# Windowed attention and routed experts on one core: ninth-block loads moved up, one transpose moved, weight splits deferred while routing

## The chip, the core and the metric

The kernel runs on one core of a Trainium2 chip. PE is the matrix engine, DVE the vector engine, ACT the scalar engine, POOL the GpSimd engine, SP the engine that issues most loads and stores. The metric is device time in microseconds of one execution; the time before is the median of three.

## The reference

Attention first: 8 batches, 8 heads, 576 positions, head size 64; a position sees itself and the 63 before it. Its output, as 4608 rows of 512, goes through a skipping mixture of 8 experts. In short:

```
scores = q @ k.T / 8, masked to 0 <= row - column < 64; attn = softmax(scores); x = attn @ v
compute = x @ w_skip > 0; rows without it are passed through
expert  = argmax(x @ w_gate); gate = softmax value of that expert
out     = x + gate * (relu(x @ w1[expert]) @ w2[expert])
```

## The kernel before, in words

**Attention.** The 576 positions of a batch are nine blocks of 64. A tile is two blocks, 128 rows; a pair of batches makes nine tiles, and the ninth of them (tiles 8, 17, 26, 35) holds the two ninth blocks. k, q and v come in groups of four blocks, half a group per load (`load_k`, `load_q`, `load_vm`); the ninth blocks of a pair come in loads of their own: two of k (`load_k_tail`, tile `kt`), one of q (`load_q_tail`, tile `qt`, L211) and one of v (`load_v_tail`, tile `vt`). Per tile PE does the scores (`score`, L244), the transposes of the softmax (`transpose_p`, L279), the product with v (`tile_out`, av, L368), the transposes of the result x (`transpose_x`, px, L323, copied to xt by ACT at L325) and the gate's logits (`logits`, L335, written over px and copied by ACT to lg, L342). DVE masks and reduces the scores and normalises x (L379 to L382), ACT makes the exponentials, POOL masks ptm. The loop over t issues score(t+1), the transposes of x of an earlier tile, and tile_out(t-1).

**Loads.** `when_at` gives each load a tile number and one of four slots in it; `feed` puts the loads of a slot in a queue, pending, when the program comes to it. `tick` counts PE's instructions; every 256 of them (BLOCK) it issues the stores of finished tiles and then up to four loads (LOADS) from pending on SP, all made to wait for that PE instruction. These are the batches spoken of below. `after_load` bounds the transfers in flight to six.

**Routing.** When the logits of a group of tiles are done (the last group is tiles 30 to 35), `route` works on it in steps that `routes` takes from the list `late`: DVE steps (gmx, gd, gfi, gfm, goh, gohb), a count by PE into a tile pr, more DVE steps, and then one scatter of list entries per tile on POOL (L553), issued by `pace`. The lists of the third item and those after it are read when all scatters have landed (`load_list`), and their rows gathered (`gather_x`, L579).

**Experts.** Rows are worked in items, each in four steps of an up product in two halves (`up`, tile p1, L797 to L799) and, two steps later, a down product (`down`). A half's result goes through ACT (hh, L843) and DVE (hl, L846). p1, px, pt and pr share one PSUM tag with two banks, taken in turn. Rows of an item are transposed in `split_x` (px2, L786; xh by ACT, xl by DVE, L790). Weights come as pieces of 128 x 1024: a raw load (L730) into one of six buffers, then a split into whi (ACT, L749) and wlo (DVE, L750); a load reuses its buffer after the wlo six pieces before. `weights_to(n)` splits up to piece n and issues the raw loads that this frees. `expert_chunk` is one call of the expert work: it first splits some weights and then takes the next chunk (a half of an up, a half of a down, or an empty one at the end of a step). Its `need` is the last piece that the next step wants. The calls are numbered here from the first one after tile_out(34). In the seam (L1068 to L1094) they alternate by hand with the last tiles of attention, and from L1258 on with the last routing steps:

```
need = max(when[part(min(k + 1, last), 0)], when[part(min(k - 1, last), 1)] if k else 0) + 1
turns[0] += 1
more = turns[0] % 2 if late else RATE
weights_to(max(need, min(ptr["split"] + more, ptr["free"] + min(RING, len(ring)) - 1)))
```

Of the kernel before, what the change touches and what calls it, by code (L numbers as in the profile page):

```python
# [24 lines left out]
NT = N // P  # L25
# [35 lines left out]
RATE = 1  # L61
# [78 lines left out]
def window_attention_moe(ctx: ExitStack, tc, a, out):  # L140
# [171 lines left out]
    def block_v(b, i):  # L312
        if i == 8:
            return vms["t", b // 2][:, b % 2]
        return vms[2 * b + i // 4][:, i % 4]
# [3 lines left out]
    def transpose_x(t):  # L319
        x = xns.pop(t)  # L320
        px = psum.tile([P, NDC, P], F32, name="px", tag="t", bufs=2)
        for c in range(NDC):
            tick(2, nc.tensor.transpose(px[:, c], x[:, c * P : (c + 1) * P], ident))  # L323
        xt = xs.tile([P, NDC, P], F32, name="xt", bufs=NXT)
        nc.scalar.copy(xt, px)  # L325
        xts[t] = px, xt

    def logits(t):

        px, xt = xts.pop(t)  # L330
        o = px[:, 0, 0:9]
        for c in range(NDC):
            for hf in range(2):
                r = slice(64 * hf, 64 * hf + 64)
                tick(4, nc.tensor.matmul(  # L335
                    o[r], xt[:, c, r], wg[:, c], start=c == 0, stop=c == NDC - 1, skip_group_check=True
                ))
        if t in heads:
            n = GRP[heads.index(t)]
            grp[:] = [t, n, sm.tile([P, n, 9], F32, name="lg")]  # L340
        t0, n, lg = grp
        nc.scalar.copy(lg[:, t - t0], o)  # L342
        if t + 1 == t0 + n:
            late.append(route(t0, n, lg))

    def tile_out(t):
        blks = tiles[t]
        ptm = pts.pop(t)
        have = {}
        for b, i in blks:  # L350
            for w in range(2):
                if i >= w and (b, i - w) not in have:
                    have[b, i - w] = block_v(b, i - w)
        win = [[have.get((b, i - w)) for w in range(2)] for b, i in blks]
        x = xs.tile([P, D], F32, name="x")
        av = pav.tile([P, 2, 512], F32, name="av")
        summing = held[0] == "sums" and (t < 26 or held[1] >= 2)
        if summing:
            held[2] = av[:, 0, 4 * VW :]
            step()  # L360
        for q in range(4):
            for w in range(2):
                for hf in range(2):
                    if win[hf][w] is None:
                        continue
                    for z in range(2):
                        h = slice(64 * z, 64 * z + 64)
                        ins = tick(4, nc.tensor.matmul(  # L368
                            av[64 * hf : 64 * hf + 64, z, q * VW : (q + 1) * VW],
                            ptm[h, q, 2 * hf + 1 - w],  # L370
                            win[hf][w][h, q],
                            start=w == 0,
                            stop=w == 1 or win[hf][1] is None,
                            skip_group_check=True,
                        ))
        feed(t + 1, 2)
        r = sm.tile([P, 2, 4], F32, name="r")
        src = av[:, :, : 4 * VW].rearrange("p z (h c) -> p z h c", c=VW)
        nc.vector.tensor_scalar(r, src[..., 64], 1e-9, None, op0=ALU.add)  # L379
        nc.vector.reciprocal(r, r)  # L380
        stores.append((x, blks))
        beat(nc.vector.tensor_tensor(  # L382
            x.rearrange("p (q z c) -> p z q c", z=2, c=64),
            src[..., 0:64],
            r.unsqueeze(3).to_broadcast([P, 2, 4, 64]),
            op=ALU.mult,
        ))
        feed(t + 1, 3)
        xns[t] = x
        progress[0] = t + 1  # L390
        while t >= NT - 2 and stores:
            store()
        return step if summing else lambda: None
# [3 lines left out]
    def store(ins=None):  # L397
        x, ((b0, i0), (b1, i1)) = stores.pop(0)
        r0 = b0 * S + i0 * 64
        r1 = b1 * S + i1 * 64  # L400
        if r1 == r0 + 64:
            done = [nc.sync.dma_start(out[r0 : r0 + P], x)]
        else:
            done = [nc.sync.dma_start(out[r0 : r0 + 64], x[:64]), nc.sync.dma_start(out[r1 : r1 + 64], x[64:])]
        if ins is not None:
            behind(done[0], ins)
            flying.append((done[0].ins, 1))
# [86 lines left out]
    def tick(n, ins):  # L494
        pe[0] += n
        if pe[0] >= pe[1]:
            pe[1] += BLOCK
            while len(stores) > SDELAY:
                store(ins)
            transfers(ins)  # L500
        return ins
# [15 lines left out]
    def beat(ins):  # L517
        beats[0] = ins.ins
# [16 lines left out]
    def feed(t, slot):  # L535
        pending.extend(at.get((t, slot), ()))
        if pe[0] < BLOCK:
            transfers()
# [133 lines left out]
    late = []  # L672
# [3 lines left out]
    def step():  # L676
        held[:2] = next(late[0], late), 0
        if held[0] is late:
            late.pop(0)
# [18 lines left out]
    part = lambda k, w: (ITEMS[steps[k][0]][2], steps[k][1], w)  # L698
# [7 lines left out]
    when = {pc: n for n, pc in enumerate(pieces)}  # L706
    ring, used = [], {}
# [12 lines left out]
    RING = 10  # L720
    ptr = {"dma": 0, "split": 0, "free": 0, "use": 0}
    wrow = {}

    def weight_dma(n):
        e, qi, w = pieces[n]
        if e not in wrow:
            r = e % E
            ix = perm[0:1, r, 2:3] if r < 2 else tables["order"][0:1, r, 1:2]
            wrow[e] = nc.values_load(ix, engines=[SP], min_val=0, max_val=(E - 1) * NQ * P)
        return nc.sync.dma_start(  # L730
            raws[n % NRAW], a["wq"][bass.ds(wrow[e] + qi * P, P), w * 1024 : w * 1024 + 1024]
        )
# [13 lines left out]
    def weight_split(n):  # L746
        hi, lo = ring[n % RING]
        raw = raws[n % NRAW]
        nc.scalar.copy(hi, raw)  # L749
        nc.vector.tensor_tensor(lo, raw, hi.bitcast(F32), op=ALU.subtract)  # L750

    def weights_to(n):
        n = min(n, len(pieces), ptr["free"] + len(ring))
        while ptr["split"] < n:
            while ptr["dma"] < min(len(pieces), ptr["split"] + NRAW):
                if not can_load(ptr["dma"]):
                    break
                weight_dma(ptr["dma"])
                ptr["dma"] += 1
            if ptr["dma"] == ptr["split"]:  # L760
                break
            weight_split(ptr["split"])
            ptr["split"] += 1
        while ptr["dma"] < min(len(pieces), ptr["split"] + NRAW) and can_load(ptr["dma"]):
            weight_dma(ptr["dma"])
            ptr["dma"] += 1
# [3 lines left out]
    def can_load(n):  # L770
        return pieces[n][0] % E < 2 or "order" in tables
# [207 lines left out]
    with tc.manual_schedule():  # L979
# [16 lines left out]
        def when_at(t, slot, f, *args):  # L996
            at.setdefault((max(t, 0), slot), []).append(functools.partial(f, *args))
# [3 lines left out]
                part2 = i // 2 % 2 if i < 4 else i - 4  # L1001
                when_at(max(first_of[n] - AHEAD, 0) + i // 3, (0, 1, 3)[i % 3], f, n, 2 * part2, 2 * part2 + 2)
        for m in range(B // 2):
            t = 9 * m + (0 if m else 2)
            when_at(t, 3, load_k_tail, m, 0)
            when_at(t + 1, 3, load_k_tail, m, 1)
            when_at(t + 2, 3, load_q_tail, m)
            when_at(t + 3, 3, load_v_tail, m)
        for t in U0:
            when_at(t, 1, weight_dma_first)  # L1010
        score(0)
# [42 lines left out]
        hpool["h"] = ml  # L1054
        chunks = expert_chunks()
        place = [0]
        turns = [0]

        def expert_chunk():
            k = place[0]  # L1060
            last = len(steps) - 1
            need = max(when[part(min(k + 1, last), 0)], when[part(min(k - 1, last), 1)] if k else 0) + 1
            turns[0] += 1
            more = turns[0] % 2 if late else RATE
            weights_to(max(need, min(ptr["split"] + more, ptr["free"] + min(RING, len(ring)) - 1)))
            place[0], c = next(chunks)

        for j, tag in enumerate("gu"):  # L1068
            its[0].split(*xhl[0], j, tag)()
        summed = tile_out(NT - 2)  # L1070
        transpose_x(NT - 3)
        logits(NT - 3)
        summed()
        pace(1)
        expert_chunk()
        masks = transpose_p(NT - 1)
        transpose_x(NT - 2)
# [7 lines left out]
        routes(1)  # L1085
        pace(1)
        expert_chunk()
        transpose_x(NT - 1)
        routes(1)
        expert_chunk()  # L1090
        logits(NT - 1)
        routes(1)
        pace(1)
        expert_chunk()  # L1094
        attn.close()
        pattn.close()
        banks["v"] = ctx.enter_context(tc.tile_pool(name="plv", bufs=1, space=PSUM, side="right", reuse_waits="tile"))
# [169 lines left out]
        while True:  # L1267
            k = place[0]
            i, qi = steps[min(k, len(steps) - 1)]
# [17 lines left out]
    more = nc.values_load(tables["left"][0:1, 0:1], min_val=0, max_val=NSLOT)  # L1287
# [71 lines left out]
```

## Time and profile before

| | us |
|---|---|
| median of three runs | 435.95 |
| the three runs | 432.66, 435.95, 436.6 |
| the profiled execution, its own device time | 433.25 |
| its span, first to last instruction | 431.6 |

The profile has one page (busy times, the span in slices, the chain that ended last, groups of instructions) and views of the trace: timelines of an engine with the idle time ahead of an instruction and what ended it in brackets, waits in total, and windows with busy times and the clock that PE was granted (1.00 is 2.4 GHz, 0.50 is 1.2 GHz). Times count from the span's start.

### The profile page before, as it was taken

To read this page: it belongs to the slowest core of one execution; us is meant where nothing else is said; L and a number is where in the kernel's file an instruction comes from. 1 tells how busy PE (TensorE), PEld (TensorE's weight loads), DVE (VectorE), ACT (ScalarE), POOL (GpSimd) and SP (SyncE) were. 2 spreads that over 40 slices of the span, in tenths; PEclk is the share of its full clock that TensorE was granted. 3 is DMA by queue.
4 is the path that set the end of the run, shared out by engine and by line. 5 is a ranking of instruction groups with operands and counts; after the bars stand their busy time and mean duration, and the time that the engine had idled before them with its cause. 6 is when DMAs were issued, how large, how long until landed. Compare 5 with 4: busy or idle time off the path is not lost.

```text
span 431.6 us, 14543 instructions
## 1 busy us (share of the span) xinstructions
PE 393.1 (91%) x5865; PEld 341.4 (79%) x5865; DVE 271.9 (63%) x558; ACT 223.0 (52%) x658; POOL 181.7 (42%) x223
## 2 busy tenths in 40 slices
PE   5887999998989888889999899999999999999980
PEld 3775888887878777877887798898898888888860
DVE  2664678878899567679216679665455466756520
ACT  3774787676758566655124536234244444444510
POOL 4552554566765584645264717025025332101010
PEclk9997999999989899999999999999999999999995
DMA  8967879879687697748557837555758776686300
GB/s 257 315 211 238 278 241 334 261 246 320 202 269 231 190 350 252 244 151 272 207 171 234 277 116 259 166 177 183 246 191 246 240 229 200 224 269 226 93 31 18
DMA packets 40757, 95.66 MB, mean 222 GB/s; under 512 B 7401, under 2 KB 9063, under 8 KB 40680
## 3 DMA queue, kind: packets, MB, share of 16 engines
q1 hardware_dynamic: 33040, 78.17, 55.6%
q0 software_dynamic: 5056, 10.02, 7.0%
q10 hardware_dynamic: 2592, 6.52, 4.5%
q8 instruction: 47, 0.77, 0.8%
q14 instruction: 22, 0.18, 0.1%
HBM read 80.55 MB, written 14.97 MB: 221 GB/s over the span
## 4 chain that ended last, share of the span: by engine, by line
PE 77%; DVE 7%; DMA 6%; issue 4%; ACT 2%; POOLq 0%; SPq 0%; ACTq 0%; DVEq 0%
PE p L797 9%; PE p L798 8%; PE p L799 8%; PE av L368 7%; PE ps L244 7%; PE px L323 4%; PE yv L797 4%; PE yv L799 4%; PE yv L798 4%; PE pt L279 4%; PE px L335 3%; PE yw L797 3%; PE yw L798 3%; PE yw L799 3%; DVE wlo L750 2%
## 5 line engine op out<-in xcount | busy, mean ns | idle before, releaser
L750 DVE TENSOR_TENSOR wlo<-raw,whi 128x1024 fp32r<-128x1024 f32 x72 | 87.8, 1225 | 23.8 <-ACT whi L749 23.5
L843 ACT ACTIVATE hh<-p 128x256 fp32r<-128x256 f32 (+4 forms) x64 | 25.0, 390 | 111.1 <-PE p L799 106.5
L797 PE MATMUL p<-xh,whi 128*128 128x256 f32 (+5 forms) x256 | 77.0, 301 | 2.7 <-DVE hl L846 2.4
L798 PE MATMUL p<-xl,whi 128*128 128x256 f32 (+5 forms) x256 | 75.3, 294 | 0.1
L799 PE MATMUL p<-xh,wlo 128*128 128x256 f32 (+5 forms) x256 | 75.1, 293 | 0.0
L749 ACT CAST whi<-raw 128x1024 fp32r<-128x1024 f32 x72 | 74.5, 1047 | 0.0
L286 POOL TENSOR_TENSOR ptm<-pm,mask 128x512 f32<-128x512 f32 x36 | 45.8, 1272 | 56.7 <-ACT pm L285 54.3
L269 ACT ACTIVATE s<-ps,nmx 128x64 f32<-128x64 f32 x288 | 66.4, 324 | 1.2
L846 DVE SCALAR_TENSOR_TENSOR hl<-p,hh 128x256 fp32r<-128x256 f32 (+4 forms) x64 | 27.3, 427 | 59.4 <-ACT hh L843 31.9
L872 POOL DMA_INDIRECT out<-yo,les x15 | 15.2, 1014 | 103.1 <-DVE yo L871 93.2
L797 PEld LDWEIGHTS p<-xh,whi 128*128 128x128 f32 x256 | 48.3, 189 | 6.1 <-DVE hl L846 3.0
L368 PE MATMUL av<-vm,ptm 64*64 64x65 f32 x2048 | 46.1, 228 | 7.4 <-issue 7.2
L553 POOL DMA_INDIRECT lists<-ent,gdi x36 | 40.6, 1129 | 24.8 <-issue 12.8
L368 PEld LDWEIGHTS av<-vm,ptm 64*64 64x64 f32 x2048 | 39.7, 139 | 13.8 <-issue 13.1
L798 PEld LDWEIGHTS p<-xl,whi 128*128 128x128 f32 x256 | 48.4, 189 | 1.4 <-DVE xl L790 0.5
L799 PEld LDWEIGHTS p<-xh,wlo 128*128 128x128 f32 x256 | 48.4, 189 | 0.0
L244 PE MATMUL ps<-k,q 64*64 64x128 f32 (+1 forms) x1024 | 40.3, 286 | 1.8 <-issue 1.7
L260 DVE COPY_PREDICATED ps<-sel,ps 128x512 f32<-128x512 int32 x36 | 25.0, 694 | 23.3 <-PE ps L244 23.1
L325 ACT COPY xt<-px 128x512 f32<-128x512 f32 x36 | 21.2, 588 | 28.5 <-PE px L323 28.4
L244 PEld LDWEIGHTS ps<-k,q 64*64 64x64 f32 x1024 | 31.3, 143 | 3.8 <-issue 3.4
L797 PE MATMUL yv<-whi,hh 128*128 128x512 f32 (+1 forms) x72 | 28.9, 402 | 0.0
L799 PE MATMUL yv<-whi,hl 128*128 128x512 f32 (+1 forms) x72 | 28.4, 394 | 0.0
(179 smaller groups left out, 735.1 us busy)
## 6 DMA issues: line engine op xcount, KB each, us to landing
raw<-wq SPq DMA_DIRECT2D x72, 512.0 KB, 5.1
vm<-vp SPq DMA_DIRECT2D x32, 260.0 KB, 5.4
q<-qT SPq DMA_DIRECT2D x32, 256.0 KB, 4.5
out<-x SPq DMA_DIRECT2D x32, 256.0 KB, 4.4
k<-kT SPq DMA_DIRECT2D x24, 256.0 KB, 4.5
w<-wq ACTq DMA_DIRECT2D x12, 512.0 KB
k<-kT SPq DMA_DIRECT2D x8, 384.0 KB, 4.5
kt<-kT SPq DMA_DIRECT2D x8, 256.0 KB, 3.3
```

Source lines behind the costliest of these rows:

```text
L244: tick(4, nc.tensor.matmul(ps[64 * hf : 64 * hf + 64, z, p, 64 * w.start :], q[h, p], k[h, w, p], start=True, stop=True, skip_group_check= ...
L260: nc.vector.copy_predicated(cur, sel.unsqueeze(1).unsqueeze(1).to_broadcast([P, 2, 4, 64]), ps[..., :64])
L269: nc.scalar.activation(s[:, q, z], cur[:, z, q], AF.Exp, bias=nmx[:, z, q : q + 1], scale=0.125)
L286: nc.gpsimd.tensor_tensor(part(0, 2), split(pm[:, 0:2], 2), kept(2), op=ALU.mult)
L368: ins = tick(4, nc.tensor.matmul(av[64 * hf : 64 * hf + 64, z, q * VW : (q + 1) * VW], ptm[h, q, 2 * hf + 1 - w], win[hf][w][h, q], start= ...
L553: ins = nc.gpsimd.indirect_dma_start(out=lists, out_offset=bass.IndirectOffsetOnAxis(ap=di, axis=0), in_=ent.bitcast(I32), in_offset=None, ...
L749: nc.scalar.copy(hi, raw)
L750: nc.vector.tensor_tensor(lo, raw, hi.bitcast(F32), op=ALU.subtract)
L797: nc.tensor.matmul(o, lh, rh, start=first, stop=False)
L798: nc.tensor.matmul(o, lh, rl, start=False, stop=False)
L799: nc.tensor.matmul(o, ll, rh, start=False, stop=last)
L846: beat(nc.vector.scalar_tensor_tensor(hl[:, f, :m], p1[:, :m], 0.0, hh[:, f, :m].bitcast(F32), op0=ALU.max, op1=ALU.subtract))
```

## The change

Three edits. The loads of the first pair's ninth blocks get due times 1, 2, 2, 3 in place of 2, 3, 4, 5. In the seam the transposes of x of tile 33 are issued ahead of tile_out(34), and an expert call that stood behind the logits of tile 35 is issued two places earlier, so that the calls from the third on stand: third, fourth, transposes of x of tile 35, fifth, logits of tile 35. And while routing is unfinished, a call splits the pieces that its own chunk needs, or one more than are split as long as that is no more than `need`.

```diff
         for m in range(B // 2):
-            t = 9 * m + (0 if m else 2)
-            when_at(t, 3, load_k_tail, m, 0)
-            when_at(t + 1, 3, load_k_tail, m, 1)
-            when_at(t + 2, 3, load_q_tail, m)
-            when_at(t + 3, 3, load_v_tail, m)
+            ts = [9 * m + i for i in range(4)] if m else [1, 2, 2, 3]
+            when_at(ts[0], 3, load_k_tail, m, 0)
+            when_at(ts[1], 3, load_k_tail, m, 1)
+            when_at(ts[2], 3, load_q_tail, m)
+            when_at(ts[3], 3, load_v_tail, m)
...
-            turns[0] += 1
-            more = turns[0] % 2 if late else RATE
-            weights_to(max(need, min(ptr["split"] + more, ptr["free"] + min(RING, len(ring)) - 1)))
+            if late:
+                now = max(when[part(min(k, last), 0)], when[part(k - 2, 1)] if k >= 2 else 0) + 1
+                weights_to(max(now, min(need, ptr["split"] + 1)))
+            else:
+                weights_to(max(need, min(ptr["split"] + RATE, ptr["free"] + min(RING, len(ring)) - 1)))
             place[0], c = next(chunks)
 
         for j, tag in enumerate("gu"):
             its[0].split(*xhl[0], j, tag)()
+        transpose_x(NT - 3)
         summed = tile_out(NT - 2)
-        transpose_x(NT - 3)
         logits(NT - 3)
...
         expert_chunk()
+        expert_chunk()
         transpose_x(NT - 1)
         routes(1)
         expert_chunk()
         logits(NT - 1)
         routes(1)
         pace(1)
-        expert_chunk()
         attn.close()
```

## Rows read from the trace of the kernel before

**Rows 1.** The page, part 1: engine, busy us, share of the span, instructions.

```profile
PE 393.1 (91%) x5865; PEld 341.4 (79%) x5865; DVE 271.9 (63%) x558; ACT 223.0 (52%) x658; POOL 181.7 (42%) x223
```

**Rows 2.** Timeline of PE, 35 to 49 us: start, duration, engine, line, instruction.

```profile
35.15 0.64 PE L335 MATMUL px<-wg,xt 128*64 128x9 f32 x16
38.95 1.99 PE L244 MATMUL ps<-kt,qt 64*64 64x128 f32 x32 [3.16 <-DMA qt<-qT]
...
45.03 1.09 PE L244 MATMUL ps<-k,q 64*64 64x128 f32 x32
...
48.74 1.10 PE L244 MATMUL ps<-k,q 64*64 64x128 f32 x32
```

**Rows 3.** Windows: length, busy us by engine, granted clock, DMA share, GB/s.

```profile
38.00:40.00 2.00, 1.05 (x20) 1.05 (x24) 0.00 (x0) 0.00 (x0) 0.00 (x0) 0.50 0.64 214
...
44.00:46.00 2.00, 2.00 (x81) 1.79 (x74) 1.06 (x3) 1.41 (x8) 1.33 (x2) 0.98 0.89 339
```

**Rows 4.** Timeline of SP's queue, 23 to 36 us.

```profile
23.17 0.35 SPq L402 DMA_DIRECT2D out<-x  x1
...
33.90 2.00 SPq L211 DMA_DIRECT2D qt<-qT  x1
```

**Rows 5.** Waits of the whole span: us in total, times, longest.

```profile
PE av L368 <- issue: 7.2, 10, 1.4
```

**Rows 6.** Timeline of PE, 141 to 149 us.

```profile
141.91 0.58 PE L368 MATMUL av<-vm,ptm 64*64 64x65 f32 x23 [1.33 <-issue]
...
142.98 1.95 PE L244 MATMUL ps<-k,q 64*64 64x128 f32 x32
...
148.32 1.10 PE L244 MATMUL ps<-k,q 64*64 64x128 f32 x32
```

**Rows 7.** Timeline of PE, 168 to 218 us.

```profile
168.41 0.64 PE L335 MATMUL px<-wg,xt 128*64 128x9 f32 x16 [0.68 <-ACT xt L325]
...
176.97 0.66 PE L323 MATMUL px<-ident,x 128*128 128x128 f32 x4 [1.01 <-DVE x L382]
...
179.88 0.39 PE L797 MATMUL p<-xh,whi 128*128 128x256 f32 x1 [0.27 <-ACT lg L342]
...
181.42 0.60 PE L786 MATMUL px<-ident,xg 128*128 128x128 f32 x4
...
185.42 0.39 PE L797 MATMUL p<-xh,whi 128*128 128x256 f32 x1 [1.75 <-DVE hl L846]
...
203.37 0.40 PE L797 MATMUL p<-xh,whi 128*128 128x288 f32 x1 [0.67 <-DVE hl L846]
...
217.75 0.60 PE L786 MATMUL px<-ident,xg 128*128 128x128 f32 x4
```

**Rows 8.** Timeline of ACT, 167 to 177 us.

```profile
167.77 0.59 ACT L325 COPY xt<-px 128x512 f32<-128x512 f32 x1
...
176.01 0.17 ACT L342 COPY lg<-px 128x9 f32<-128x9 f32 x1 [1.29 <-PE px L335]
```

**Rows 9.** Timeline of DVE, 182 to 203 us.

```profile
182.04 0.42 DVE L846 SCALAR_TENSOR_TENSOR hl<-p,hh 128x256 fp32r<-128x256 f32 x1
182.38 0.20 DVE L424 SCALAR_TENSOR_TENSOR gfi<-gd,cf 128x48 f32<-128x48 f32 x1
...
183.22 0.68 DVE L790 TENSOR_TENSOR xl<-px,xh 128x512 fp32r<-128x512 f32 x1
183.82 1.22 DVE L750 TENSOR_TENSOR wlo<-raw,whi 128x1024 fp32r<-128x1024 f32 x1
...
199.50 3.49 DVE L750 TENSOR_TENSOR wlo<-raw,whi 128x1024 fp32r<-128x1024 f32 x3
```

**Rows 10.** Timeline of POOL, 182 to 215 us: scatters to the lists, a gather of rows.

```profile
182.74 0.97 POOL L553 DMA_INDIRECT lists<-ent,gdi  x1 [1.55 <-DVE gfi L424]
184.01 1.86 POOL L553 DMA_INDIRECT lists<-ent,gdi  x1 [0.30 <-DVE xl L790]
...
214.09 1.09 POOL L579 DMA_INDIRECT xg<-out,les  x1 [0.91 <-DMA raw<-wq]
```

More of the change, by code (lines that the diff above doesn't have):

```diff
@@ L1056, in window_attention_moe @@
         place = [0]
-        turns = [0]
         def expert_chunk():
```

## The prediction

> **What bounds the kernel now.** I began with the page: PE is busy 91% of the span [rows 1], so time is won only where PE stands still or runs slowly. After it I read PE's own timeline with its idle times, the clock by windows, and then the queue or engine that each idle time names. Three places matter for this change.
>
> First, the ninth blocks. PE ends the logits at 35.79 and starts the scores of tile 8 at 38.95, 3.16 us later, released by the load of qt [rows 2]. It then works at a granted clock of 0.50, the 1.2 GHz level, and has 0.98 again in the window from 44 on [rows 3]. From 38.95 to the next tile's scores pass 6.08 us, from those to the next 3.71 [rows 2]. SP issues qt at 33.90 [rows 4], and PE starts 5.05 us after that.
>
> Second, the seam between attention and experts. PE stands 0.68 us before the logits of tile 33, 1.01 before the transposes of x of tile 35, 0.27 before the second half of the experts' second step, 1.75 before the second half of the third [rows 7]. Third, an echo of that seam: 0.67 at 203.37, released by DVE's hl [rows 7], which stands behind three wlo of 3.49 us together [rows 9].
>
> **The change part by part.** *Loads of the first pair.* The queue is filled by the counted instructions of PE: a batch takes the stores that are due and up to four loads. Going through the counts with the new due times, the batch behind the store at 23.17 [rows 4] is now v, v, kt, qt (it was v, kt), the next vt, k, q (it was kt, k, q), the one of the old qt k, q, v, v. From the batch at tile 10's scores on all are as before. So qt moves two batches forward, to between 24 and 28. With the same 5.05 us it lands by 33, and PE wants it at 35.79: some 3 us of cover. No load is added. What goes back in the queue is the v of tiles 6 and 7, by a batch or less; PE wants it after 38.
>
> What it saves: the wait of 3.16, and the slow stretch behind it, 6.08 - 3.71 = 2.37; together 5.53. What is late next: k and q of tiles 9 and 10, which PE now wants 5.5 us sooner, at about 39.5 and 43.2 (before: 45.03 and 48.74 [rows 2]). Those of tile 9 stay in the batch ahead of the old qt: issued before 33.90 and with its 5.05 us they are there by 38.95. q of tile 10 followed the old qt at once, so it is issued by 36.4 at the latest and there by 41.5. Cover is left, so no new wait stands in the sum. The price: the batch at 23.17 has five transfers where it had three. PE has ten stops in av with no releaser but "issue", 7.2 us in all, the longest 1.4 [rows 5], and more of them may come in fuller batches. From below it is -0.7 (one stop of the mean length vanishes), from above a stop of 1.33 as at 141.91 with a slow stretch: 142.98 to 148.32 is 5.34 where 3.71 is normal, 1.63 more, 2.96 together [rows 6]. I take +0.4, half a mean stop, since the rows with such stops are few. Sum of this part: -5.1.
>
> A rule bears on those stops. The Trainium skill's page "Runtime: NRT & Kernel Launch", section "Instruction fetch mechanics", says that a sequencer fetches its next page while it works on the current one, at a cost mostly hidden. If the stops are such fetches, by that rule the +0.4 would be nothing and the sum 0.4 us lower; the stop of 1.33 speaks for a cost that isn't always hidden, and no row names its cause.
>
> *x of tile 33 ahead of av of tile 34.* PE's four transposes come some 1 us sooner. But the logits of tile 33 wait for xt [rows 7], which ACT copies at 167.77 with no idle time ahead of it [rows 8]: ACT is held by casts that stand before it in its program, and their order is not changed. So xt ends at 168.36 and the logits start at 168.41 as before; PE's idle time only changes its place. I count 0. Bounds: 0.7 gained (the whole wait), 0.3 lost if the av, now later, holds up r and x of tile 34 on DVE.
>
> *The seam, third and fourth call.* Both now stand ahead of the transposes of x of tile 35. The third issues no matmul, only a split; the fourth is the first half of the second step. The two PSUM banks of the shared tag keep alternating: this half takes the bank of tile 34's logits, free when ACT's lg copy ends at 176.18 [rows 8]. It starts at 176.25, takes 1.54 (179.88 to 181.42 [rows 7]), and the transposes fill PE to 178.2. The second half needs hl of the first; with DVE free, an hl ends 1.04 us after its half (181.42 to 182.46 [rows 7, 9]). So it starts at 178.85 in place of 179.88: -1.03. The logits of tile 35 follow it, to 180.95, some 1.4 us later than before, and with them the last group's routing.
>
> *Splits only as needed.* While routing is unfinished, the old code splits a weight in every odd call; the new one only what the step at hand needs, and one more up to the next step's need. Call by call: splits 1 to 4 stay; split 5 goes from the seventh call to the eighth, split 6 from the ninth to the eleventh, 7 to 14 one call later each; from the nineteenth call on both are equal. The first half of the third step then runs from 181.35 to 182.9, and its hl no longer has wlo 5 (1.22 at 183.82 [rows 9]) ahead of it: 182.9 + 1.04 is 183.94. DVE has six small steps of routing before it, from 181.5 on, some 0.23 each as the 0.20 at 182.38, and xl of 0.68 [rows 9]: they end at 183.5 and fit. The second half starts at 183.95 in place of 185.42: -1.47 at this point, the 1.03 in it. Up to the 0.67 PE's timeline shows no further gap. That one goes too: its hl has one wlo fewer ahead, and DVE enters the stretch 1.5 us sooner, so hl ends near 200.9 and PE asks at 201.0. What hides the later splits is DVE's lead: in the worst case a piece is split some 5 us before use, and a late one would cost its 1.22. No DMA is added; a raw load follows its wlo as before. Sum of the seam: -1.47 - 0.67 = -2.1, between 0 (DVE loses elsewhere what it saves here) and -3.7 (1.01, 0.27, 1.75 and 0.67 all go).
>
> A second rule of the Trainium skill, "SBUF — State Buffer", section "Who interferes with whom": a DVE instruction with two SBUF inputs contends with a GpSimd instruction that reads SBUF. wlo is one; a scatter of list entries took 0.97 at 182.74 and 1.86 at 184.01, 0.19 after a wlo began [rows 9, 10], so the trace agrees, with 0.89 us. By my count about as many wlo as before fall on the last six scatters, so the rule leaves the sum; as a danger it is rival (b).
>
> *Sum.* The profiled execution's own time is 433.25 (span 431.6, 1.65 around it): -5.1 - 0 - 2.1 gives 426.05. The median of the runs is 435.95; the four executions known (432.66, 433.25, 435.95, 436.6) have their middle at 434.6, and 434.6 - 7.2 = 427.4 is my forecast. After 204 I expect no loss: PE is the bound there.
>
> **The rivals.** (a) The wait is replaced in part, by a stop with a slow stretch, 2.96 [rows 6], or by k or q of tile 9 coming late. One of these leaves 7.6 - 3.0 = 4.6 of gain: 430.0. For it: five transfers in the new batch and covers of 0.5 to 3 us. Against: the few stops in all of attention [rows 5]. (b) The seam gives nothing, because the list chain sets what follows it: the third item's rows are gathered at 214.09 [rows 10] and PE transposes them at 217.75 [rows 7], with little to spare. If the last six scatters took 0.89 more each, 5.3 in all, PE would wait for what it had won, 2.1: 429.5. (c) The change does not do what it says: qt stays behind the loads ahead of it, lands only by 38, and the slow stretch stays; 1 us and the seam remain: 431.5. (d) Slower: the stops grow with the fuller batches. Each costs 2.96; three eat all 7.6 of gain. It decides from the third on; with five (each batch from 23 to 42) the kernel stands at 434.6 - 7.6 + 14.8 = 441.8.
>
> **How the numbers follow.** The forecast has 0.53, (a) 0.20, (b) 0.12, (c) 0.08, (d) 0.07. A measurement of this kernel tells about 1% (4.4 us) from no change; its runs span 3.9. Below 431.6 lie nearly all of the forecast and of (b) and half of (a) and (c): 0.75. Slower by over 1%: most of (d), 0.05. Within: 0.20. The range runs from 423.0 (no new stop, the seam's whole 3.7, and a run as fast as 432.66 was before) to 432.5 (past (a), (b) and (c)).
>
> **What would show it.** Right: the scores of tile 8 start within 0.5 us of the logits before them, no window from 36 to 44 has a clock near 0.5, and a tile takes about 3.7 there. Some 0.7 to 1.0 of waiting stays before the logits of tile 33. The second step's first half starts right behind the lg copy; the 1.75 falls below 0.8; the 0.67 is gone. Wrong: a wait of 1 us or more on k, q or "issue" where 23 to 45 stood, a wlo right ahead of an hl that PE waits for, or a wait before the third item's transposes.

## The result, and the profile after

The changed kernel takes 428.68 us (median of ten runs, 425.92 to 431.65); the kernel before, run again beside it, takes 433.50 (ten runs, 431.63 to 438.66). The ratio is 0.9883 [0.9841, 0.9925]: 4.8 us by the medians, 5.1 by the ratio, where 7.2 were forecast; it is faster by over 1%, though the interval reaches to 0.75%. The time lies only 1.3 us from the forecast of 427.4, and that is partly luck: the gain came out 2.4 us short, and the kernel before 1.1 us below the 434.6 that the forecast was counted from. Ratios compare the fast executions of two kernels (one over 1.5% above the fastest of its kernel counts as slow), and the profiles of e1, e7 and e12 below are of slow ones. The profiled execution of the changed kernel took 431.65 and was the slowest of its ten, so what follows compares stretches, not spans.

The page of the changed kernel, parts 1 and 3. It answers to [rows 1]; q8 is a queue of the kind "instruction", with packets of 16 KB.

```profile
PE 390.9 (91%) x5865; PEld 339.6 (79%) x5865; DVE 273.8 (64%) x558; ACT 223.6 (52%) x658; POOL 181.2 (42%) x223
...
q1 hardware_dynamic: 33040, 78.17, 55.6%
...
q8 instruction: 47, 0.77, 0.8%
```

PE's timeline of the changed kernel, which answers to [rows 2] and [rows 7]:

```profile
35.25 0.64 PE L335 MATMUL px<-wg,xt 128*64 128x9 f32 x16
35.82 1.10 PE L244 MATMUL ps<-kt,qt 64*64 64x128 f32 x32
...
39.56 0.50 PE L244 MATMUL ps<-k,q 64*64 64x128 f32 x10
41.62 1.10 PE L244 MATMUL ps<-k,q 64*64 64x64 f32 x22 [1.55 <-issue]
...
46.65 1.10 PE L244 MATMUL ps<-k,q 64*64 64x128 f32 x32
...
153.12 1.10 PE L244 MATMUL ps<-k,q 64*64 64x128 f32 x32 [0.56 <-DMA q<-qT]
...
160.03 1.10 PE L244 MATMUL ps<-kt,qt 64*64 64x128 f32 x32 [1.55 <-DMA qt<-qT]
...
169.09 0.64 PE L335 MATMUL px<-wg,xt 128*64 128x9 f32 x16 [0.94 <-ACT xt L325]
...
178.26 0.60 PE L323 MATMUL px<-ident,x 128*128 128x128 f32 x4
179.63 0.39 PE L797 MATMUL p<-xh,whi 128*128 128x256 f32 x1 [0.78 <-DVE hl L846]
...
184.85 0.39 PE L797 MATMUL p<-xh,whi 128*128 128x256 f32 x1 [0.76 <-DVE hl L846]
```

The 3.16 before the scores of tile 8 are gone: they start right behind the logits. But one tile on, PE stops for 1.55 us in the middle of the scores of tile 9 (10 of 32 matmuls stand before the stop), and the slow stretch comes there. Windows of the changed kernel (length, busy us of PE, PEld, DVE, ACT and POOL, granted clock, DMA share, GB/s), beside [rows 3]:

```profile
38.00:40.00 2.00, 2.00 (x92) 1.83 (x92) 1.66 (x5) 1.96 (x11) 1.51 (x2) 1.00 0.90 259
40.00:42.00 2.00, 0.45 (x18) 0.39 (x18) 0.24 (x1) 0.66 (x4) 0.44 (x1) 1.00 1.02 365
42.00:44.00 2.00, 2.00 (x22) 1.67 (x15) 1.21 (x2) 0.20 (x1) 0.00 (x0) 0.53 0.86 301
44.00:46.00 2.00, 2.00 (x67) 1.67 (x65) 0.60 (x2) 1.65 (x8) 0.84 (x1) 0.61 0.82 263
46.00:48.00 2.00, 2.00 (x63) 1.74 (x55) 1.22 (x4) 1.32 (x7) 1.11 (x2) 1.00 0.45 164
```

The clock is at 0.53 and 0.61, near its 1.2 GHz level, in the four microseconds after a window in which PE was busy for 0.45; before, it was 0.50 after the wait for qt. In the seam the 1.01, the 0.27 and the 0.67 of [rows 7] are gone and the 1.75 is 0.76, but a new 0.78 stands before the second step's second half. The engine behind both is DVE. Its timeline in the changed kernel has the third step's hl (184.37) ahead of the wlo, where [rows 9] have the wlo first; but the second step's hl, the one behind the 0.78, still stands right behind a wlo:

```profile
177.96 1.28 DVE L750 TENSOR_TENSOR wlo<-raw,whi 128x1024 fp32r<-128x1024 f32 x1 [0.25 <-ACT whi L749]
179.16 0.41 DVE L846 SCALAR_TENSOR_TENSOR hl<-p,hh 128x256 fp32r<-128x256 f32 x1
...
184.37 0.42 DVE L846 SCALAR_TENSOR_TENSOR hl<-p,hh 128x256 fp32r<-128x256 f32 x1 [0.21 <-ACT hh L843]
185.31 1.23 DVE L750 TENSOR_TENSOR wlo<-raw,whi 128x1024 fp32r<-128x1024 f32 x1 [0.51 <-ACT whi L749]
```

To place the gain, each trace is cut in three by two events of PE: A from the start to the transposes of x of tile 34 (171.96 before, 172.76 after), B from there to the first quad product of the second item (yu, a part of its down product; 215.48 before), C from there to the end. B is 43.52 before and 40.99 after; C is 216.12 and 216.15. So the seam won 2.5 us and nothing was lost behind it. A is no such clean number: over the traces of this study it lies between 167.4 and 182.5, and two traces of the changed kernel differ by 5.4 us there (172.76, and 167.35 in e6 below). What is left of the medians' 4.8 for A is 2.3.

### The profile page after: what moved, and what is told of

Its sections match the earlier page's. It is cut to its first block, busy times and chain, and to the rows that moved or that the text cites. A ratio compares the mean times of both kernels' runs of the same rounds, so it can differ in the third digit from the quotient of the medians.

```text
span 429.9 us, 14544 instructions
## 1 busy us (share of the span) xinstructions
PE 390.9 (91%) x5865; PEld 339.6 (79%) x5865; DVE 273.8 (64%) x558; ACT 223.6 (52%) x658; POOL 181.2 (42%) x223
## 4 chain that ended last, share of the span: by engine, by line
PE 81%; DMA 6%; issue 4%; ACT 3%; DVE 3%; POOLq 0%; SPq 0%; ACTq 0%; DVEq 0%
PE p L797 9%; PE av L368 9%; PE p L798 8%; PE p L799 8%; PE ps L244 7%; PE px L323 4%; PE px L335 4%; PE yv L797 4%; PE yv L799 4%; PE yv L798 4%; PE pt L279 4%; PE yw L797 3%; PE yw L798 3%; PE yw L799 3%; PE px L786 2%
## 5 line engine op out<-in xcount | busy, mean ns | idle before, releaser
L368 PEld LDWEIGHTS av<-vm,ptm 64*64 64x64 f32 x2048 | 40.2, 140 | 14.5 <-issue 14.1
L244 PE MATMUL ps<-k,q 64*64 64x128 f32 (+1 forms) x1024 | 38.8, 281 | 4.0 <-issue 3.3
```

The lines of the kernel that those rows point to most:

```text
L244: tick(4, nc.tensor.matmul(ps[64 * hf : 64 * hf + 64, z, p, 64 * w.start :], q[h, p], k[h, w, p], start=True, stop=True, skip_group_check= ...
L368: ins = tick(4, nc.tensor.matmul(av[64 * hf : 64 * hf + 64, z, q * VW : (q + 1) * VW], ptm[h, q, 2 * hf + 1 - w], win[hf][w][h, q], start= ...
```

## The experiments

Theory at the start: the seam is worth 2.5 us, made by the calls and the splits; the transposes of tile 33 add nothing; the loads take the wait away and get a stop with its slow stretch back. Rivals: the stop is chance and the loads are worth 5; or one of the calls and splits makes all of the seam.

**The parts by themselves** (12 runs each; the ratios rest on 11, 8, 4 and 10 of them, in order).

e1, against the kernel before, is the new due times alone:

```diff
-            t = 9 * m + (0 if m else 2)
...
+            ts = [9 * m + i for i in range(4)] if m else [1, 2, 2, 3]
...
```

e2 is the rest: the same lines the other way round, against the changed kernel. e3, against the kernel before, is the call issued earlier alone:

```diff
         expert_chunk()
+        expert_chunk()
         transpose_x(NT - 1)
...
-        expert_chunk()
         attn.close()
```

e4, against the kernel before, is the rule of the splits alone:

```diff
-            turns[0] += 1
-            more = turns[0] % 2 if late else RATE
...
+            if late:
+                now = max(when[part(min(k, last), 0)], when[part(k - 2, 1)] if k >= 2 else 0) + 1
+                weights_to(max(now, min(need, ptr["split"] + 1)))
...
```

> The kernel before with the loads' edit alone. Theory 1 (the waits add up as forecast): the wait for qt and the slow stretch behind it go, 5.5 us, and are kept to the end: 5.1 us faster than before, ratio about 0.988. Theory 2 (given back): the time won at tile 8 is lost again before 165 us to stops of PE with the releaser issue and to waits for loads: 2.4 us faster, ratio about 0.9945. In both, the profile shows no wait for qt at tile 8; theory 2 wants a stop of over 1 us with a slow clock behind it between 38 and 66 us.

> The kernel before with the seam's edits alone (transposes of x of tile 33 moved, calls moved, split rule). Theory 1: 2.1 us faster, ratio 0.995. Theory 2, from the whole change's 4.8 us less 2.4 for the loads: 2.4 us faster, ratio 0.9945, so about as much as the loads. The wait of 3.16 for qt at tile 8 stands in the profile. If the seam alone gave under 1 us, the loads would carry the whole gain.

> The kernel before with the call moved and the old split rule. By the forecast's working the move is worth 1.03 us at the second half of the second step; the old rule still splits a piece right ahead of the third step's hl, so the wait there stays long (over 1.3) and the 0.67 near 203 stays: 0.5 to 1.0 us faster, ratio 0.998. The rival, that the move is worth nothing because the last routing starts later, says 0 or slower.

> The kernel before with the new split rule and the old order of calls. By the forecast the wait of 1.75 ahead of the third step's second half falls by about 1.0 (one wlo of 1.22 less ahead of its hl) and the 0.67 near 203 goes: 1.1 to 1.7 us faster, ratio 0.9965. The 1.01 ahead of the transposes of x of tile 35 stays. The rival (a postponed wlo comes due elsewhere) says no gain and a new wait for hl between 190 and 205.

| | ratio | B | C |
|---|---|---|---|
| e1 loads | 0.9962 [0.9912, 1.0012] | 43.49 | 216.18 |
| e2 seam | 0.9898 [0.9843, 0.9954] | 40.98 | 216.18 |
| e3 calls | 0.9919 [0.9848, 0.9990] | 43.23 | 216.14 |
| e4 splits | 1.0010 [0.9963, 1.0056] | 42.48 | 218.07 |

PE's timeline with the loads alone:

```profile
37.85 1.10 PE L244 MATMUL ps<-kt,qt 64*64 64x128 f32 x32
...
43.37 0.88 PE L244 MATMUL ps<-k,q 64*64 64x64 f32 x22 [1.28 <-issue]
...
165.22 1.99 PE L244 MATMUL ps<-kt,qt 64*64 64x128 f32 x32 [2.40 <-DMA qt<-qT]
```

PE's timeline with the seam alone:

```profile
39.17 1.75 PE L244 MATMUL ps<-kt,qt 64*64 64x128 f32 x32 [3.38 <-DMA qt<-qT]
...
178.71 0.39 PE L797 MATMUL p<-xh,whi 128*128 128x256 f32 x1 [0.77 <-DVE hl L846]
...
183.92 0.39 PE L797 MATMUL p<-xh,whi 128*128 128x256 f32 x1 [0.76 <-DVE hl L846]
```

The loads alone remove the wait for qt, and the stop stands in the same place as in the whole change; their gain is 0.4%, with no change inside the interval and the forecast's 0.988 outside it. The seam alone gives the whole 2.5 of B (its ratio says 4.5 us, with an interval from 2.0 to 6.9). Of the parts of the seam, the calls alone win 0.29 in B, the splits alone 1.04, both together 2.5: each needs the other. With the calls alone the third step's wait is 1.85, for the wlo still stands ahead of the hl; the ratio of that run is better than its trace can explain, it rests on four executions, and I go by the trace. The splits alone lose 1.95 in C, more than they win in B, and PE waits there for the third item's rows. Their wait at the third step is 0.71, as forecast (1.75 less about 1.0); the 0.67 at 203, which they were to take away, stays (0.73 at 206.04). PE's timeline with the splits alone:

```profile
188.06 0.39 PE L797 MATMUL p<-xh,whi 128*128 128x256 f32 x1 [0.71 <-DVE hl L846]
...
222.24 0.66 PE L786 MATMUL px<-ident,xg 128*128 128x128 f32 x4 [1.68 <-DMA xg<-out,les]
```

**The seam without the moved transposes** (one execution), and **the changed kernel again**. The edit of the first, against the changed kernel (its loads are also as before):

```diff
-        transpose_x(NT - 3)
         summed = tile_out(NT - 2)
+        transpose_x(NT - 3)
```

> The whole seam without the move of the transposes of x of tile 33, and without the loads' edit. From the transposes of x of tile 34 to the first quad product of the second item the kernel before takes 43.52 us, the whole seam 40.98, the moved call alone 43.23, the split rule alone 42.48. If the move of the transposes is worth nothing, as forecast, this takes 40.98 again, and the wait ahead of the logits of tile 33 is 0.68 in place of 0.94. If the move carries part of the 2.5, it takes more: the two single parts sum to 42.2.

> The changed kernel once more, beside the next two. Theory 2 (the time won at tile 8 is given back before 165 us) wants the transposes of tile 12 about 3 us sooner than in the kernel before (61.5), those of tile 27 less than 1.5 us sooner (125.9), and from tile 34 to the first quad product 40.98 us again. Theory 1 wants 4 us or more kept at tile 27. In time: ratio near 0.988.

Without the move B is 41.01, as with it (40.98, 40.99), and the wait before the logits of tile 33 is 0.68 in place of 0.94. So the move is worth nothing. The changed kernel again gives 0.9861 [0.9800, 0.9922]. B is 41.35, 0.4 over what was expected; no row gives the reason. Against the one trace of the kernel before, it is 3.0 us ahead at 61.5 and 3.2 at 125.9, and the first profile of the changed kernel 2.6 and 0.3: neither theory's sign (under 1.5 or 4 and more at 125.9) holds in both. The stop in the scores of tile 9 comes a second time:

```profile
41.20 0.88 PE L244 MATMUL ps<-k,q 64*64 64x64 f32 x22 [1.21 <-issue]
```

**Is the stop made by a batch of loads just ahead of a fetch?** `FETCH` is the count of PE instructions at which the first batch falls; every later one follows 256 on. Two kernels shift all batches against the packets of instructions.

```diff
-FETCH = 200
+FETCH = 24
```

That is e7; e8 has 136.

> The changed kernel with each batch of stores and loads issued 80 PE instructions later (the count starts at 24 in place of 200). In the traces a packet of the instruction queue ends 1.2 to 1.6 us before each stop with the releaser issue is over, and these packets begin about 1 us behind a batch. If the stops are instruction fetches that stand in line behind the batch's loads, the batch now begins behind the fetch and the fetches have the quieter end of the loads: stops before 172 us fall from 11.2 in all to under 7, and the kernel is 2 to 5 us faster than the changed one. If the stops come from the loads' total rate and not from the order, they stay at 9 to 15 and the time stays within 1 us.

> The changed kernel with each batch issued 64 PE instructions sooner (the count starts at 136). If the stops are fetches behind a batch's loads, the loads of a batch are then under way for some 2 us when the fetch begins, about the fullest point: stops of 11 us in all or more, time the same or up to 3 us slower than the changed kernel. If only the total rate counts, no difference from the changed kernel beyond 1 us.

e7: 0.9969 [0.9935, 1.0003] to the kernel before, so slower than the changed kernel (e6, beside it: 0.9861), which neither branch of the expectation has; no row tells why. Its stops of "issue" before 172 us add up to 14.5 us in 15, where under 7 were expected and the changed kernel has 11.1 in 12. e8: 1.0131 [1.0063, 1.0199], with 11.3 us of stops, as expected, but far more than 3 us slower than the changed kernel. A q comes late in it: the 31st load of q goes out behind the lists, at 153.67, where the changed kernel issues it ahead of them, at 136.71. PE's timeline of e8:

```profile
157.34 1.99 PE L244 MATMUL ps<-k,q 64*64 64x128 f32 x32 [5.93 <-DMA q<-qT]
```

The idea falls as it was stated: the stops did not shrink. Whether the place of a batch counts for less than that can't be said, since a single trace tells little here: e1 and e12, one and the same kernel, have 15.1 and 7.2 us of stops.

**Is it the loads around the stop?** e9 leaves out the two loads of v of group 4 and uses v of group 1 in its place, e10 makes them due one tile later. Against the changed kernel, e9:

```diff
+                if n == 4 and i >= 4:
+                    continue
...
-        return vms[2 * b + i // 4][:, i % 4]
+        n = 2 * b + i // 4
+        return vms[1 if n == 4 else n][:, i % 4]
```

and e10:

```diff
-                when_at(max(first_of[n] - AHEAD, 0) + i // 3, (0, 1, 3)[i % 3], f, n, 2 * part2, 2 * part2 + 2)
+                when_at(max(first_of[n] - AHEAD, 0) + i // 3 + (n == 4 and i >= 4), (0, 1, 3)[i % 3], f, n, 2 * part2, 2 * part2 + 2)
```

> The changed kernel without the two loads of v of tiles 9 and 10 (520 KB that stood in the batch at 32.5 us); these two tiles use the v of tiles 2 and 3, so their rows of the output and what is routed from them are other than the reference's. Times after 60 us are not compared. In all three traces with the loads' edit PE stops at tile 9's scores (1.55, 1.21 and 1.28 us at 41 to 43 us) behind an instruction packet that took 2.5 us among the loads. If the loads' crowd there makes the stop, it falls under 0.6 us here and the transposes of the seventh tile in order start near 45.5, not 47.3 to 48.1, against 49.8 in the kernel before: the full gain of the wait. If the stop comes with PE's order alone, it stays over 1.2 us.

> The changed kernel with the same two loads due one tile later, so that the batch at 32.5 us has two loads and the next one four. Nothing is left out. If the crowd between 34 and 40 us makes the stop, spreading it by one tile halves the stop (0.3 to 0.8 us) and wins 1 to 3 us against the changed kernel: ratio to the kernel before 0.980 to 0.986. If the total rate sets it, the stop only moves one tile on, and the ratio is that of the changed kernel, 0.986 to 0.988.

PE's timeline of e9 (nothing behind 60 us is compared):

```profile
40.63 1.18 PE L244 MATMUL ps<-k,q 64*64 64x128 f32 x32
...
46.61 1.09 PE L244 MATMUL ps<-k,q 64*64 64x128 f32 x15 [1.43 <-issue]
```

In e9 the stop is out of tile 9 and comes one tile on, with 1.43, and the transposes of the seventh tile start at 47.63, not near 45.5. Loads moved by a tile change nothing that can be told: 0.9852 [0.9794, 0.9909] holds both branches of the expectation, and the stop at 41.19 of 1.17 is not halved. So the stop does not hang on when these two loads go out. That leaving them out moved it is not shown by one trace: e12 below has almost no stop in tile 9 with all loads in place. (The expectation of e9 has one slip: of the three packets it speaks of, one took 2.52 us, the others 2.22 and 1.85.)

**The last pair's ninth blocks.** In the profiles with the new loads, q or qt of the last pair came late. e11 makes the last pair's loads due sooner; e12 is the loads alone once more, for a second profile of that part.

```diff
-            ts = [9 * m + i for i in range(4)] if m else [1, 2, 2, 3]
+            ts = {0: [1, 2, 2, 3], 3: [26, 26, 26, 27]}.get(m, [9 * m + i for i in range(4)])
```

> The changed kernel with the ninth blocks of the last pair loaded sooner too (due 26, 26, 26, 27 in place of 27, 28, 29, 30). In four of eight traces PE waits 1.4 to 2.4 us for qt at tile 35 or 0.5 to 0.6 for a q before it, near 153 to 165. If that wait goes and is kept, the gain over the changed kernel is about 1 us on the mean of runs and the ratio 0.983 to 0.987; if the loads that it displaces (q and v of the last groups) are late in its place, or the seam takes it back, no difference from the changed kernel.

> The loads' edit alone once more, since the first measurement left it between 0.9912 and 1.0012. The forecast's term of 5.1 us says 0.988. The traces so far say that from the transposes of the fourth tile in order to those of the seventh the kernel before takes 14.8 to 16.7 us, the kernels with this edit 12.9 to 15.8, so 1.6 us less on the mean: ratio 0.996. A stop with the releaser issue of over 1 us between 40 and 47 us is expected again.

PE's timeline of e11, with SP's loads of qt and of the 31st q ahead of it:

```profile
130.60 1.11 SPq L211 DMA_DIRECT2D qt<-qT  x1
...
148.30 0.42 SPq L201 DMA_DIRECT2D q<-qT  x1
...
151.77 1.99 PE L244 MATMUL ps<-k,q 64*64 64x128 f32 x32 [5.70 <-DMA q<-qT]
```

PE's timeline of e12:

```profile
39.40 0.88 PE L244 MATMUL ps<-k,q 64*64 64x64 f32 x22 [0.39 <-issue]
...
153.17 1.10 PE L244 MATMUL ps<-k,q 64*64 64x128 f32 x32 [1.65 <-DMA q<-qT]
...
160.38 1.98 PE L244 MATMUL ps<-kt,qt 64*64 64x128 f32 x32 [2.79 <-DMA qt<-qT]
```

e11 takes 0.9952 [0.9914, 0.9991], no better than the changed kernel (0.9883 [0.9841, 0.9925]) and likely slower: qt goes out at 130.60 where it was 152.45, the 31st q at 148.30, behind the lists, where it was 136.71, and PE waits 5.70 for a q. e12 takes 0.9941 [0.9871, 1.0012], which excludes neither 0.988 nor 0.996. Its stop was only 0.39, which I had not expected, and from the fourth to the seventh transposes of x it takes 3.6 us less than the mean of the traces with the old loads; at 153 and 160 it waits 4.4.

None of the twelve beats the changed kernel beyond its interval.

## Why the prediction was right, and which term was wrong

The measured time lies in the range, and the gain of 4.8 us is that of rival (a), 4.6, rather than the forecast's 7.2. Two of the signs that the prediction gave for being wrong were met: a stop of over 1 us on "issue" ahead of 45 us, with a clock of 0.53 in the window from 42 on, and a wlo right ahead of an hl that PE waits for.

**The wait for qt** went as worked out. qt is issued at 26.51, where "between 24 and 28" was forecast; the scores of tile 8 start with no wait. SP's timeline of the changed kernel, which answers to [rows 4]; the later rows are for what follows below:

```profile
26.08 0.38 SPq L208 DMA_DIRECT2D kt<-kT  x1
26.51 0.42 SPq L211 DMA_DIRECT2D qt<-qT  x1
...
140.83 1.86 SPq L664 DMA_DIRECT2D es<-lists  x2
142.90 1.89 SPq L657 DMA_DIRECT2D es<-lists  x4
...
152.45 0.39 SPq L211 DMA_DIRECT2D qt<-qT  x1
```

**The price of the loads was mis-sized.** The step that failed is "I take +0.4, half a mean stop, since the rows with such stops are few". Its upper bound of 2.96 is what came in the changed kernel: rival (a), a stop with a slow stretch. In the scores of tile 9 there is a stop of 1.55, 1.21, 1.28, 1.17 and 2.49 us in five of the six profiles that have the new loads, all of v and the old `FETCH` (in the order after, e6, e1, e10, e11); only e12 has a small one, 0.39. None of the five traces with the old loads has a stop between 36 and 50 us. The slow stretch is not always there: behind the stops of after, e6 and e11 the granted clock falls to 0.50 to 0.53 in a window of 2 us, behind those of e1 and e10 it stays at 1.00. The window behind e6's stop of 1.21, and the one behind e1's of 1.28:

```profile
42.00:44.00 2.00, 2.00 (x14) 1.66 (x16) 1.39 (x2) 0.58 (x1) 0.00 (x0) 0.52 0.87 284
...
44.00:46.00 2.00, 2.00 (x66) 1.66 (x66) 1.39 (x3) 1.12 (x4) 0.18 (x1) 1.00 1.00 334
```

From the fourth to the seventh transposes of x the old loads take 16.0 us (mean of five traces, 14.8 to 16.7), the new ones 13.9 (mean of those six, 12.4 to 15.8); three tiles of 3.72 are 11.2. So the term of -5.1 was some -2.1 here (-1.6 without e1 and e12). The two traces of the changed kernel stand at 14.6 and 14.2, 3.4 and 3.0 above the 11.2, which is the 2.96 of the bound; e1, e10 and e12, without the slow stretch, at 1.2 to 2.0 above it.

I looked at the stops of PE in av alone [rows 5]. The same view of the changed kernel, and then the row of the scores in the kernel before:

```profile
PE av L368 <- issue: 7.6, 9, 1.6
...
PE ps L244 <- issue: 3.3, 2, 1.7
...
PE ps L244 <- issue: 1.7, 4, 0.8
```

The total in av is about as before (7.2); the new stop stands under the scores.

What a stop is can be read from the records of PE and of the instruction queue. In the fourteen traces PE has 154 stops of "issue" of 0.3 us or more before 172 us, and in each of them it goes on 1.1 to 1.6 us after a packet of q8 has ended. They also stand at fixed places of the program: counted through PE's matmuls, weight loads and the few other records of its queue, the instruction behind each of the 154 stops stands 193 or 194 behind a multiple of 256, and q8 has 47 packets for PE's 11,860 records, one for every 252. So a stop is PE without instructions until the next packet is in.

One such place lies in the scores of tile 9, behind 10 of the 32 matmuls, and the place before it in the scores of tile 8. Each line has the time at which PE passes the place before; start, time and end of the packet between the two; when PE goes on at the place in tile 9 and how long it stood there; and the time from place to place without the stop:

```
before   39.03   39.32  0.88  40.20   45.26  no stop   6.23
e2       39.24   39.35  0.89  40.24   44.70  no stop   5.46
after    35.89   37.76  2.52  40.27   41.62  1.55      4.18
e6       35.82   37.75  1.85  39.60   41.20  1.21      4.18
e1       37.92   39.59  2.22  41.81   43.37  1.28      4.18
e10      35.80   38.95  0.88  39.83   41.19  1.17      4.22
e11      37.04   41.33  0.88  42.21   43.76  2.49      4.23
e12      34.83   36.89  0.88  37.77   39.40  0.39      4.18
```

In the kernel before, PE passes the first place only after its wait for qt and comes to the second at half clock, 6.23 us later; the packet was in by 40.20. With the wait gone PE runs at full clock and is there after 4.18 us, before the packet is in. That the loads' edit brings the stop is shown by the traces without it, which have none here, against e1, e12 and the four others. How long the stop is depends on when the packet starts, 1.7 to 4.3 us after PE has passed the first place, and on what it takes, 0.88 to 2.52. Loads under way are not enough for a slow packet. In the changed kernel the other queue fills the DMA engines; its transfers by queue from 36 to 42 us (packets, MB, share of the 16 engines):

```profile
q1 hardware_dynamic: 928, 1.83, 95.4%
q8 instruction: 1, 0.02, 2.6%
```

But in e12 q1 has 96.7% in the same stretch, and the packet took 0.88. The rule that the prediction weighed there, of the Trainium skill's page "Runtime: NRT & Kernel Launch", section "Instruction fetch mechanics", says a fetch is mostly hidden; the traces disagree with it here: all stops of "issue" before 172 us sum to 7.2 to 15.1 us in the fourteen traces, 9.2 before and 11.1 after.

**A second piece is given back at the last pair.** Four of the five profiles that have the new loads and leave the later ones alone wait for q or qt between 148 and 165 us; with the old loads it is one of five (without e1 and e12, two of three against one of five). SP's rows above say what goes ahead of it: es, the first lists, are loaded at 140.83 where it was 138.16, and qt goes out at 152.45 where it was 149.33. SP stands there until the scatters have landed. Its waits in the changed kernel have a row for it that the kernel before has not:

```profile
SPq L664 <- DMA lists<-ent,gdi: 2.3, 1, 2.3
```

This wait of SP and PE's wait for q and qt behind it go together in all ten profiles with unchanged later loads and `FETCH`:

```
               before   e2    e4    e5    e6   e10   e3   after   e1   e12
SP, for lists    0      0     0     0     0    1.1   2.3   2.3   2.9   3.0
PE, for q, qt    0      0     0     0    0.2   1.9   2.0   2.1   2.9   4.4
```

That the new loads cause it is not shown: e3 has it with the old loads and e6 lacks it with the new ones. Nor does the changed kernel's trace show PE sooner there: its 27th transposes of x start at 136.85, in the kernel before at 134.95, and the last scatter ahead of the lists at 136.1 against 134.3. SP's wait is over 3.6 us after that scatter's end, while in the kernel before 2.8 us were enough for it to have landed; why it lands later is open. e11, made to take the wait away, only brought another load late.

**The seam** was forecast at 2.1 and gave 2.5. Taken from the end of the logits' copy, the second half of the second step was forecast at 2.67 (178.85 against 176.18); it starts 2.65 behind it (179.63 against 176.98). The second half of the third step was forecast at 7.77 and starts at 7.87. The wait at 203 is gone, as forecast. PE's idle time in B fell from 3.70 (1.01, 0.27, 1.75, 0.67) to 1.54 (0.78, 0.76): 2.16; the other 0.4 has no row. Of the 0.78 that is left at the second step some 0.3 is the wlo of 177.96 ahead of its hl: hh is done at 178.85, hl starts at 179.16. What I did not say is that neither edit gives its part alone.

**The moved transposes** are worth 0, and the wait before the logits of tile 33 is 0.94, within the 0.7 to 1.0 given.

**The rivals.** (b), the third item's rows, did not come in the changed kernel: its six last scatters take 8.06 us together, 8.05 before. But its rows land only 0.12 us before PE takes them (0.20 before), so nothing more is to be won ahead of them on PE alone. With the splits alone PE does wait for them, 1.68, and not for the reason given: the six scatters take 8.07 there, but the gather starts 13.7 us after the last of them, not 12.5, and lands 0.8 later behind its start. The contention itself is there, and the order decides it. Of the scatters of all fourteen traces that begin 0.08 us or more into a wlo with no second wlo right behind it, each of 82 ends 0.84 to 0.94 us after that wlo; each of 35 with a wlo that begins after it takes 0.97 to 1.01, such as the one at 185.05 with the wlo of 185.31 above:

```profile
185.05 0.97 POOL L553 DMA_INDIRECT lists<-ent,gdi  x1 [0.30 <-DVE hl L846]
```

(c) is out by the issue at 26.51. (d) is out: the stops grew by 1.9 us, within what traces of one kernel differ by, and not by three stops with their slow stretches.

## What to carry to other kernels

A wait that goes may have covered another: before its whole price is counted, look at which engine or queue was catching up behind it, the instruction queue among them, and put the full upper bound in the sum where one of that queue's places lies close behind; here such places stand 256 instructions apart and can be counted in advance. Edits in one seam can need each other, so price the pair, then each alone. And where the early part of a kernel varies by several microseconds between executions, measure an edit by a stretch between two events, not by the span.

## What the runs showed of the hardware that was not expected

The instructions themselves come by DMA, and PE runs dry for 7 to 15 us of the first 172 us in every trace, always at the same places of its program, 256 instructions apart. Shifting the batches of loads, thinning them or moving them by a tile changed at which of these places it stops, and no variant was shown to lessen the sum. A slow packet is not the whole of it: in e9, e10 and e11 the stop followed a packet of 0.88 us that had begun late, 3.2 to 4.3 us after PE had passed the place before. Why a packet begins late is open; none of the runs tells it. And a stop of 1.2 or 1.3 us has the half clock behind it in some traces (e6) and not in others (e1, e10).
